# State read-outs of two batches at a time, and the last sum and stores of a fused attention and MLP kernel, on one core

## The chip, the core and the metric

The kernel runs on one core of a Trainium2 chip. The core has five engines that run side by side, each with its own queue of instructions: TensorE (PE; its weight loads are shown apart as PEld), VectorE (DVE), ScalarE (ACT), GpSimd (POOL) and SyncE (SP), which here only issues DMAs. The metric is the device time of one execution in microseconds (us). Three runs of the kernel before took 205.12, 204.68 and 204.35 us, median 204.68.

## What is computed

```python
# x: (8, 8, 512, 64) = (B, H, S, D); state: (8, 8, 32, 64) = (B, H, Ns, D)
a     = softmax(scale * x @ state.T)        # per token over the 32 states
xread = a @ state                           # (B, H, 512, 64)
a2    = softmax(scale * state @ x.T)        # per state over the 512 tokens
sread = a2 @ x                              # (B, H, 32, 64)
rows  = concat([xread, sread], axis=2)      # (B, H, 544, 64), heads then side by side: 4352 x 512
out   = gelu(rows @ w_in) @ w_out           # w_in 512 x 2048, w_out 2048 x 512
```

So there are per batch 512 token rows and 32 state rows. In the text, "state read-out" is sread: for each state a sum over the tokens of its batch, weighted with the exponentials.

## The kernel before, in words

The eight batches pass one after the other through a software pipeline that is written out by hand: instructions run on each engine in the order in which the program lists them, and the pools only add waits for buffers. For batch b the loop at line 1140 has eight slots p of two hidden tiles each; "slot 2" and the like in the diff's summary means the turn of the outer loop with b = 2, and its read-out stands at p = 5.

- **Tokens.** `scores` (L333, exponentials L340 into e), `norm` (L353 to L356, three DVE steps, the last one a product that writes a) and a DMA transpose (`atr_dma`) make the attention weights of batch b + 1 while batch b's MLP runs. `p_mm` (L441) multiplies state and w_in beforehand into P, so that gelu's argument is a product of a and P (`mm1`, L506, gelu at L513).
- **Second MLP product.** Per batch it is done by Strassen's scheme: seven products named "1" to "7" (`X`, matmuls at L623) in four PSUM banks, with sums of gelu outputs as weights (`g_sum`, L613, tile gsum, from a pool of three buffers) and sums of w_out as the other side. The results are put together by DVE adds (L642) into the halves oh, and stored by SP (`x_out`, L637). "7" is followed by the adds `c22` and `c21`, "3" by an add of its own.
- **State read-out.** At p = 5, behind X(b - 1, "3"), `p_all` runs `reads_mm` for the listed batches: 32 small matmuls per batch (L887) of e with xo, a copy of x with columns of ones for the denominators. ScalarE copies the result (sraw, L895). Then come the 32 matmuls of P for the next batch (L441), ScalarE and DVE copy the pieces of P (L925), and DVE normalises the read-out (`reads_norm`, L903 and L904, into srm). At p = 7 `srts` transposes srm on TensorE (L424) and a DVE copy puts it into XSR (L429). Batches 0 and 1 are read out before the loop; in the loop one batch is read out in each of the turns b = 2 to 5, and two, 6 and 7, in b = 6.
- **GpSimd.** It loads x (`load_x`, tile xb), makes a rearranged copy x4 for the transposes (`rearr`, L225) and the copy xo (`rearr_ones`, L235), two instructions each. xo and x4 have two buffers each, for odd and even batches. A `hold_for` is a copy of one column of a gelu output, which keeps what follows on GpSimd back until that output is there.
- **The state rows.** When all of XSR is there (b = 7), their MLP is done by the same scheme in `SR` and `R`, threaded through the last turns; R ends with adds into osb (L642) and two stores (`r_out`, L838). For SR, the weight sums of "1" and "6" are put in the two x4 buffers.
- **The end.** For batch 7 the products "5" and "3" come last, each in three pieces in PSUM banks of their own (`L5`, `L3`, matmuls at L701): tokens j = 0 whole, j = 1 in two halves. Each piece is copied or added and stored (`rows_out`, L687). The list ahead of them is:

```python
    g_sum(b, "7")
    R("7")
    X(b, "6")
    g_sum(b, "3")
    R("3")
    X(b, "7")
    c21(b)
    x_out(b, 1, left)
    L5()
    L3()
```

Of the kernel before, what the change touches and what calls it, by code (L numbers as in the profile page):

```python
# [10 lines left out]
BF16 = mybir.dt.bfloat16  # L11
# [6 lines left out]
def kernel(  # L18
# [8 lines left out]
    nc = tc.nc  # L27

    B, H, S, D = x.shape
# [15 lines left out]
    apool = ctx.enter_context(tc.tile_pool(name="apool", bufs=3))  # L45
# [36 lines left out]
    x4s = [persist.tile([128, SJ, HC, 128], BF16, name=f"x4_{i}") for i in range(2)]  # L82
# [32 lines left out]
    def load_x(b):  # L115
        xb = xin.tile([128, H, SJ * D], BF16, name="xb", tag="xb")
        nc.gpsimd.dma_start(out=xb, in_=xr[b])
        xbs[b] = xb
# [111 lines left out]
    def rearr_ones(b):  # L230
        A = atts[b]
        eng = nc.vector if b < 2 else nc.gpsimd
        src = xbs[b].rearrange("p (t c) (j d) -> p t c j d", t=2, d=D)
        for t in range(2):
            eng.tensor_copy(  # L235
                out=A.xo[:, :, :, 2 + 64 * t:66 + 64 * t].rearrange("p j c d -> p c j d"),
                in_=src[:, t],
            )
# [182 lines left out]
    def srts(bs):  # L421
        ps = ps_f.tile([128, len(bs), HC, NS], BF16, name="srT", tag="f")
        for i, b in enumerate(bs):
            nc.tensor.transpose(  # L424
                ps[:, i].rearrange("p c n -> p (c n)"),
                atts[b].srm.rearrange("q t d -> q (t d)"),
                ident,
            )
        nc.vector.tensor_copy(  # L429
            out=XSR[:, :, :, bs[0]:bs[-1] + 1], in_=ps.rearrange("p b c n -> p c n b")  # L430
        )
# [125 lines left out]
    MH = MC // 2  # L557
    NH = d_model // 2
# [23 lines left out]
    left, right = slice(0, NH), slice(NH, d_model)  # L582
# [8 lines left out]
    def g_q(b, h, k):  # L591
        return gs[b][:, MH * k:MH * k + MH, 256 * h:256 * h + 256]
# [12 lines left out]

    g_lhs = {}

    def g_sum(b, names):
        got = g_lhs.setdefault(b, {})
        for name in names:  # L610
            x, y, op = chain(name, lambda h, k: g_q(b, h, k), got)
            got[name] = apool.tile([128, MH, 256], BF16, name="gsum", tag="gsum")
            nc.vector.tensor_tensor(out=got[name], in0=x, in1=y, op=op)  # L613

    def x_lhs(b, name):
# [68 lines left out]
    def rows_out(h, js, ns, eng):  # L684
        b = B - 1
        rows = out[b * SB:b * SB + S, :].rearrange("(p j) n -> p j n", j=SJ)
        eng.dma_start(  # L687
            out=rows[:, 2 * h + js.start:2 * h + js.stop, ns], in_=xs[b, "o", h][:, js, ns]
        )
# [21 lines left out]
    def L5():  # L711
        b = B - 1
        xs[b, "s5"] = c_tile("s5")
        for ps, j, n0, n1 in l_mm("5", True):
            nc.scalar.copy(out=xs[b, "s5"][:, j, n0:n1], in_=ps)
            if n1 == NH:
                c22(b, slice(j, j + 1))
                rows_out(1, slice(j, j + 1), right, nc.sync)

    def L3():  # L720
        b = B - 1
        for ps, j, n0, n1 in l_mm("3", False):
            add(xs[b, "o", 0][:, j, NH + n0:NH + n1], ps, xs[b, "u"][:, j, n0:n1])
            rows_out(
                0, slice(j, j + 1), slice(NH + n0, NH + n1), nc.scalar if n0 else nc.sync
            )

    sr = {}
# [151 lines left out]
    def reads_mm(bs):  # L880
        sr = ftile([128, len(bs), 2, 65], "sr")
        for i, b in enumerate(bs):
            A = atts[b]
            for t in range(2):
                for j in range(SJ):
                    for c in range(HC):
                        nc.tensor.matmul(  # L887
                            sr[32 * c:32 * c + 32, i, t, :],
                            lhsT=A.e[:, 2 * j + t, 32 * c:32 * c + 32],
                            rhs=A.xo[:, j, c, 1 + 65 * t:66 + 65 * t],  # L890
                            start=(j == 0),
                            stop=(j == SJ - 1),
                        )
        raw = cpool.tile([128, len(bs), 130], FP32, name="sraw", tag="sraw")
        nc.scalar.copy(out=raw, in_=sr.rearrange("q i t d -> q i (t d)"))  # L895
        return raw

    def reads_norm(bs, raw):
        for i, b in enumerate(bs):
            A = atts[b]  # L900
            A.srm = att.tile([128, 2, D], BF16, name="srm", tag="srm")
            inv = att.tile([128, 2], FP32, name="inv", tag="inv")
            nc.vector.reciprocal(out=inv, in_=raw[:, i, 0:130:129])  # L903
            nc.vector.tensor_tensor(  # L904
                out=A.srm,
                in0=raw[:, i, 1:129].rearrange("q (t d) -> q t d", t=2),
                in1=inv[:, :].to_broadcast((128, 2, D)),
                op=ALU.mult,
            )

    def p_all(nb, bs):
        raw = reads_mm(bs)
        done = []
        for f, at in enumerate(((0, None), (None, None), (1, 3), (2, None))):
            it = iter(at)

            def tiles(shape, name):
                i = next(it)
                return ftile(shape, name) if i is None else otile(shape, name, i)

            done.append((nb, f, p_mm(nb, f, tiles)))
        for b, f, ps in done:
            for t in range(2):
                copy = nc.scalar.copy if t == 0 or f == 0 else nc.vector.tensor_copy
                copy(out=Ps[b][:, t, f * 512:(f + 1) * 512], in_=ps[t])  # L925
        reads_norm(bs, raw)

    def p_copy_s(b, f, ps):
        for t in range(2):
# [6 lines left out]
    def hold_for(b, m):  # L936
        nc.gpsimd.tensor_copy(out=hold, in_=gs[b][:, m, 0:1])
# [202 lines left out]
    for b in range(2, B):  # L1140
        nb = b + 1
        for p in range(8):
            k = 16 * b + 2 * p
            if p == 1 and nb < B:
                scores(nb, 0)
                scores(nb, 1)
            if p in (2, 3) and nb < B and (b > 2 or p == 2):
                norm(nb, p - 2)
            if p == 3 and nb + 1 < B:
                xtr_dma(nb + 1)  # L1150
            if p == 5 and nb < B:
                atr_dma(nb)
            if nb == B and p < 5:
                read_out_slot(p)
                if p == 4:
                    r_homes()
                    r_sum("56")
                continue
            if b != 2 or p != 3:
                M(k, k + 1)  # L1160
            if b == 2 and p == 2:
                M(k + 2, k + 3)
            if b == 2 and p == 1:
                w_diff("7")
            if p < 5 and nb < B:
                if p == 0:
                    g_sum(b - 1, "56")
                if p == 2:
                    g_sum(b - 1, "7")
                if p == 3:  # L1170
                    g_sum(b - 1, "3")
                if p < 4:
                    X(b - 1, "1657"[p])
                if b == 2 and p == 2:
                    norm(3, 1)
                    for x in [(2, f, p_mm(2, f, ftile)) for f in (2, 3)]:
                        p_copy(*x)
                if p == 1 and b > 2:
                    sr_w("5216"[b - 3])
            if p == 0 and b + 3 < B:  # L1180
                hold_for(b, 0)
                load_x(4 if b == 2 else b + 3)
            if p == 6 and b == 2:
                hold_for(b, 12)
                load_x(5)
            if p == 0 and nb + 1 < B:
                begin(nb + 1)
                rearr(nb + 1)
            if nb == B:
                if p == 5:  # L1190
                    R("2")
                    r_sum("73")
                    R("4")
                if p == 6:
                    R("1")
                    X(b, "2")
                    R("6")
                    R("5")
                if p == 7:
                    X(b, "4")  # L1200
                continue
            if p == 5:
                X(b - 1, "3")
                reads = (b, nb) if nb == B - 1 else (b,)
                p_all(nb, reads)
                if b == 2:
                    rearr_ones(3)
                    rearr_ones(4)
                elif nb + 1 < B:
                    rearr_ones(nb + 1)  # L1210
                X(b, "2")
            if p == 7:
                srts(reads)
                X(b, "4")
    b = B - 1
    g_sum(b, "56")
# [1 line left out]
    g_sum(b, "7")  # L1218
    R("7")
    X(b, "6")  # L1220
    g_sum(b, "3")
    R("3")
    X(b, "7")
    c21(b)
# [33 lines left out]
```

## Time and profile before

| | |
|---|---|
| median of three runs | 204.68 us |
| the profiled execution: its own time | 204.74 us |
| its span in the trace | 202.8 us |
| granted clock of TensorE, mean | 0.998 |
| PE busy | 194.0 us (96%) |
| ACT busy | 142.8 us (70%) |
| DVE busy | 140.4 us (69%) |
| POOL busy | 49.9 us (25%) |
| stores in the span | 8.91 MB written |

The page's part 4 follows the work that ended last back to the start; its shares tell which engine and which line set the time. The chain in order of time gives start, length and line of each piece of it. A timeline lists the instructions of a window: start, length, engine, line, operation, output and input, count, and in brackets how long the engine sat idle before it and what released it. "SPq" and "ACTq" rows are DMA issues; a DMA's landing is counted from its issue. Merged rows that hold several instructions run from the first one's start to the last one's end.

### The profile page before, as it was taken

What the parts mean: (1) busy time and instruction counts of PE and PEld (TensorE: products, weight loads), DVE (VectorE), ACT (ScalarE), POOL (GpSimd) and SP (SyncE); (2) the same over time, 40 slices, a digit from 0 to 9 for tenths busy, and PEclk for the clock granted to TensorE, in tenths of its full rate; (3) what the DMA queues carried; (4) which work ended last, traced back from release to release, by engine and by line L of the source; (5) the groups of instructions that cost most, each with busy time, mean ns of one, the idle gap of its engine ahead of it and who ended that gap; (6) DMA issues with size and microseconds to landing.
All of it is one profiled execution on the core that took longest, in us unless ns stands there. A gap on an engine that the chain in (4) does not pass through costs nothing.

```text
span 202.8 us, 4863 instructions
## 1 busy us (share of the span) xinstructions
PE 194.0 (96%) x2030; PEld 134.0 (66%) x2035; DVE 140.4 (69%) x235; ACT 142.8 (70%) x260; POOL 49.9 (25%) x63
## 2 busy tenths in 40 slices
PE   7799999999999999999999999999999999999990
PEld 2434544465767677767767677768767888788890
DVE  2953874889987579656996687567846787862760
ACT  3785578698994989678966896779758588555110
POOL 8963503324318434032306100400000000000000
PEclk9999999999999999999999999999999999999999
DMA  6999999987486999460997051701092010210125
GB/s 191 200 169 203 206 199 192 177 161 137 62 144 126 187 110 182 125 160 0 118 143 210 2 121 38 207 3 53 0 132 81 0 52 3 103 55 0 52 74 190
DMA packets 40582, 23.16 MB, mean 114 GB/s; under 512 B 21872, under 2 KB 39152, under 8 KB 40560
## 3 DMA queue, kind: packets, MB, share of 16 engines
q0 software_dynamic: 13984, 8.10, 29.6%
q1 hardware_dynamic: 25888, 14.36, 29.4%
q10 hardware_dynamic: 688, 0.39, 0.6%
q8 instruction: 16, 0.26, 0.5%
q14 instruction: 6, 0.05, 0.1%
HBM read 17.30 MB, written 8.91 MB: 129 GB/s over the span
## 4 chain that ended last, share of the span: by engine, by line
PE 87%; DMA 4%; POOL 4%; ACT 2%; issue 1%; DVE 0%; ACTq 0%; POOLq 0%
PE xp L623 41%; PE hp L506 27%; DMA w_in_bf<-in_moe_w_in_dram 4%; PE op L548 4%; PE sp L791 3%; PE rp L857 3%; PE op L532 2%; PE xp L701 2%; PE p_ps L441 2%; PE pt L333 2%; POOL w_in_bf L105 2%; ACT P L925 1%; PE sr L887 1%; POOL sbd L95 1%; POOL w_out_bf L113 1%
## 5 line engine op out<-in xcount | busy, mean ns | idle before, releaser
L513 ACT ACTIVATE g<-hp 128x512 bf16<-128x512 f32 x124 | 65.8, 608 | 13.7 <-PE hp L506 13.5
L506 PE MATMUL hp<-AT,P 128*128 128x512 bf16 x248 | 61.0, 379 | 0.0
L623 PEld LDWEIGHTS <-gsum 128*128 128x128 bf16 x416 | 40.5, 98 | 9.4 <-issue 0.4
L623 PE MATMUL xp<-ws,gsum 128*128 128x256 bf16 x320 | 38.2, 273 | 0.0
L506 PEld LDWEIGHTS <-P 128*128 128x128 bf16 x248 | 23.4, 98 | 20.8 <-issue 0.6
L623 PEld LDWEIGHTS <-g 128*128 128x128 bf16 x336 | 32.5, 98 | 7.1 <-issue 1.6
L623 PE MATMUL xp<-w_out_bf,g 128*128 128x256 bf16 x224 | 26.7, 272 | 0.3
L235 POOL COPY xo<-xb 128x1024 bf16<-128x1024 bf16 x12 | 13.2, 1127 | 36.3 <-PE sr L887 36.3
L613 DVE TENSOR_TENSOR gsum<-g 128x2048 bf16<-128x2048 bf16 x14 | 17.1, 1220 | 5.1 <-ACT g L513 4.5
L225 POOL COPY x<-xb 128x1024 bf16<-128x1024 bf16 x12 | 12.4, 1066 | 18.5 <-DMA xb<-in_x_dram 18.5
L646 ACT COPY c<-xp 128x512 f32<-128x512 f32 x14 | 8.3, 593 | 8.9 <-ACT g L513 3.9
L623 PE MATMUL xp<-ws,g 128*128 128x256 bf16 x112 | 13.4, 273 | 0.0
L642 DVE TENSOR_TENSOR oh<-xp,c 128x512 f32<-128x512 f32 x14 | 9.6, 685 | 5.4 <-PE xp L623 5.4
L925 ACT CAST P<-p_ps 128x512 bf16<-128x512 f32 x25 | 12.7, 606 | 0.1
L642 DVE TENSOR_TENSOR oh<-xp,u 128x512 f32<-128x512 f32 (+2 forms) x9 | 5.1, 572 | 10.6 <-PE xp L623 10.4
L548 PE MATMUL op<-w_out_bf,g 128*128 128x512 bf16 x44 | 11.1, 380 | 0.5 <-issue 0.3
L623 PE MATMUL xp<-w_out_bf,gsum 128*128 128x256 bf16 x96 | 11.5, 273 | 0.0
L613 DVE TENSOR_TENSOR gsum<-g,gsum 128x2048 bf16<-128x2048 bf16 x7 | 9.1, 1298 | 2.8 <-PE xp L623 2.8
L356 DVE TENSOR_TENSOR a<-e,ics 128x512 bf16<-128x512 bf16 x14 | 10.5, 750 | 0.5
L925 DVE CAST P<-p_ps 128x512 bf16<-128x512 f32 x15 | 9.4, 684 | 1.7 <-PE p_ps L441 1.7
L353 DVE TENSOR_REDUCE cs<-e 128x16 f32<-128x512 bf16 x14 | 9.5, 678 | 0.7 <-ACT e L340 0.7
L441 PE MATMUL p_ps<-w_in_bf,sbd 64*32 64x512 bf16 x248 | 9.2, 380 | 0.2 <-DMA w_in_bf<-in_moe_w_in_dram 0.2
(136 smaller groups left out, 248.6 us busy)
## 6 DMA issues: line engine op xcount, KB each, us to landing
xb<-in_x_dram POOLq DMA_DIRECT2D x7, 512.0 KB, 7.0
out_dram<-oh SPq DMA_DIRECT2D x14, 256.0 KB, 2.7
out_dram<-oh SPq DMA_DIRECT2D x6, 512.0 KB, 2.9
w_in_bf<-in_moe_w_in_dram POOLq DMA_DIRECT2D x6, 256.0 KB, 12.3
out_dram<-osb SPq DMA_DIRECT2D x5, 256.0 KB, 3.0
w_out_bf<-in_moe_w_out_dram POOLq DMA_DIRECT2D x4, 256.0 KB, 9.0
w_out_bf<-in_moe_w_out_dram POOLq DMA_DIRECT2D x2, 512.0 KB, 12.7
x0f<-in_x_dram SPq DMA_DIRECT2D x3, 256.0 KB, 3.8
```

The lines of the kernel that those rows point to most:

```text
L225: nc.gpsimd.tensor_copy(out=A.x4[:, :, :, 64 * t:64 * t + 64].rearrange("p j c d -> p c j d"), in_=src[:, t],)
L235: eng.tensor_copy(out=A.xo[:, :, :, 2 + 64 * t:66 + 64 * t].rearrange("p j c d -> p c j d"), in_=src[:, t],)
L353: nc.vector.reduce_sum(out=cs, in_=e4, axis=AX.X)
L356: nc.vector.tensor_tensor(out=A.a[:, :, hs].rearrange("p g (c n) -> p g c n", n=NS), in0=e4, in1=ics[:, :, :].to_broadcast((128, G, 2, NS) ...
L441: nc.tensor.matmul(ps[t][32 * c:32 * c + 32, :], lhsT=sbd[64 * t:64 * t + 64, b, c, 32 * t:32 * t + 32], rhs=w_in_bf[64 * t:64 * t + 64, c ...
L506: nc.tensor.matmul(hp, lhsT=Ps[b][:, t, m * 128:(m + 1) * 128], rhs=atts[b].AT[:, :, t, :], start=(t == 0), stop=(t == 1),)
L513: nc.scalar.activation(out=gs[b][:, m, :], in_=hp, func=AF.Gelu)
L548: nc.tensor.matmul(ops[b, j], lhsT=gs[b][:, m, j * 128:(j + 1) * 128], rhs=w_out_bf[:, m, :], start=(m == 0), stop=(m == MC - 1),)
L613: nc.vector.tensor_tensor(out=got[name], in0=x, in1=y, op=op)
L623: nc.tensor.matmul(ps[:, j - js[0], :], lhsT=lhs[:, m, 128 * j:128 * j + 128], rhs=rhs[:, m, :], start=(first and j == js[0] and m == 0), ...
L642: nc.vector.tensor_tensor(out=out, in0=x, in1=y, op=ALU.add)
L925: copy(out=Ps[b][:, t, f * 512:(f + 1) * 512], in_=ps[t])
```

## The change

- The read-outs in the loop are done for two batches at a time: (2, 3) in b = 2, (4, 5) in b = 4, (6, 7) in b = 6. In b = 3 and b = 5 there is none, and no transposes at p = 7.
- Batch 3's copy xo is now listed at p = 1 of b = 2, behind a hold on batch 2's gelu tile 2, instead of behind `p_all`. On GpSimd it still comes directly behind the x4 copies of batch 4, with the hold between.
- In the end, the sum for product "3" of batch 7 is written into x4's buffer 0 instead of a gsum buffer.
- The store of the right half behind `L5` is one of two tokens (256 KB) on SP instead of two of one token. Of the three stores of `L3`, the first and the last go out on ScalarE's queue and the second on SP; before, the first two went out on SP and the last on ScalarE's queue.

```diff
-    def g_sum(b, names):
+    def g_sum(b, names, home=None):
...
-            got[name] = apool.tile([128, MH, 256], BF16, name="gsum", tag="gsum")
+            if home is None:
+                got[name] = apool.tile([128, MH, 256], BF16, name="gsum", tag="gsum")
+            else:
+                got[name] = home
             nc.vector.tensor_tensor(out=got[name], in0=x, in1=y, op=op)
...
             if n1 == NH:
                 c22(b, slice(j, j + 1))
-                rows_out(1, slice(j, j + 1), right, nc.sync)
+        rows_out(1, slice(0, 2), right, nc.sync)
...
             rows_out(
-                0, slice(j, j + 1), slice(NH + n0, NH + n1), nc.scalar if n0 else nc.sync
+                0,
+                slice(j, j + 1),
+                slice(NH + n0, NH + n1),
+                nc.sync if j == 1 and n0 == 0 else nc.scalar,
             )
...
     def p_all(nb, bs):
-        raw = reads_mm(bs)
+        raw = reads_mm(bs) if bs else None
...
-        reads_norm(bs, raw)
+        if bs:
+            reads_norm(bs, raw)
...
+            if p == 1 and b == 2:
+                hold_for(b, 2)
+                rearr_ones(3)
...
-                reads = (b, nb) if nb == B - 1 else (b,)
+                reads = (b, nb) if b % 2 == 0 else ()
                 p_all(nb, reads)
                 if b == 2:
-                    rearr_ones(3)
                     rearr_ones(4)
...
             if p == 7:
-                srts(reads)
+                if reads:
+                    srts(reads)
                 X(b, "4")
...
-    g_sum(b, "3")
+    g_sum(b, "3", x4s[0].rearrange("p j (u c) n -> p (j u) (c n)", u=2))
```

## The prediction, made before the changed kernel ran

> **What bounds it now.** I read the page's parts 1 and 4 first, then the chain in order of time over one state read-out of one batch (slot 3) and over one of two batches (slot 6), then the timeline of the last 9 us, and last the timeline of POOL beside DVE.
>
> ```profile
> PE 87%; DMA 4%; POOL 4%; ACT 2%; issue 1%; DVE 0%; ACTq 0%; POOLq 0%
> ```
>
> TensorE is 87% of the chain that ends last. So an edit counts only where it lengthens or shortens TensorE's row of matmuls, or the end, where TensorE has stopped (197.99 us) and the span still runs to 202.8. The chain leaves TensorE inside the slots at one place, the read-out:
>
> ```profile
> 86.84 0.43 PE sr L887 x29
> ...
> 87.35 0.27 ACT sraw L895
> 87.62 0.58 ACT P L925
> 88.19 0.04 issue
> 88.23 1.91 PE xp L623 x16
> ```
> ```profile
> 150.48 0.67 PE sr L887 x57
> ...
> 151.23 0.38 ACT sraw L895
> 151.60 0.50 ACT P L925
> ...
> 152.14 1.91 PE xp L623 x16
> ```
>
> TensorE's next product (X "2") waits until ScalarE has copied the read-out (sraw) and then the first piece of P. From the first sr to X "2" it is 1.39 us for one batch, 1.66 for two. In slot 2 (65.57 to 67.02) it is 1.45, and there the chain goes through p_ps: 0.41 for its first 8 matmuls, 0.04, 0.59 of ACT P, 0.04 = 1.09 without any sr or sraw in it. That 1.09 is my row for a slot with no read-out. The end of the kernel:
>
> ```profile
> 194.48 1.23 DVE L613 TENSOR_TENSOR gsum<-g,gsum 128x2048 bf16<-128x2048 bf16 x1 [2.82 <-PE xp L623]
> ...
> 195.62 0.42 DVE L642 TENSOR_TENSOR osb<-rp,r_u 128x256 f32<-128x256 f32 x1
> 195.96 0.68 DVE L642 TENSOR_TENSOR oh<-xp,c 128x512 f32<-128x512 f32 x1
> ...
> 196.07 0.55 SPq L838 DMA_DIRECT2D out_dram<-osb  x1
> ...
> 197.12 0.39 SPq L637 DMA_DIRECT2D out_dram<-oh  x1
> ```
> ```profile
> 197.62 1.92 SPq L687 DMA_DIRECT2D out_dram<-oh  x4
> 198.01 0.29 DVE L642 TENSOR_TENSOR oh<-xp,u 128x128 f32<-128x128 f32 x1 [0.15 <-PE xp L701]
> 198.34 0.37 ACTq L687 DMA_DIRECT2D out_dram<-oh  x1
> ```
>
> The sum for product "3" waits 2.82 us for X "7", whose buffer it reuses. Two adds and two 256 KB stores queue behind it, so SP, at about 0.5 us per issue, sends its last piece (64 KB) at 199.1, although its add was done at 197.86. It lands 2.4 later, at 201.5. From 198.0 to 200.6 the DMA engines are full (share 1.01, 346 GB/s).
>
> **The tail.** In a buffer of its own the sum needs only gsum "6", so DVE runs it behind the two osb adds that end at 191.66: 191.66 to 192.89. R3 has finished by 192.70, so the osb add ends at 193.3 and its store leaves there, not at 196.07. c21 then waits only for X "7" (194.44): 194.48 to 195.17, and its store leaves at 195.2, not 197.12. The two c22 adds stay where they are, since they wait for ScalarE's copies (the last ends at 196.52): 196.98. Their stores are now one of 256 KB on SP at 197.0. The first add of product "3" ends at 197.63 and goes out on ACT's queue, the second at 197.86 on SP, the third at 198.30 (it waits for TensorE's end) on ACT at 198.34. So the last issue moves from 199.1 to 198.34, worth 0.8. L3's matmuls gain nothing, as TensorE runs L5 and L3 without a gap already.
>
> Landing. The 256 KB store issued alone at 189.89 shows data from 190.7 to 191.55 and lands 2.1 after issue, so about 0.9 before and 0.45 behind the data. After the change 0.52 MB are issued from 197.0 on; at 346 GB/s that is 1.5 us from 198.0, and the last 64 KB cannot start before 199.3 and needs 0.2. So the data end at 199.6 and land between 200.0 and 200.2. The same 64 KB on ACT's queue landed 2.5 after issue under full engines: 200.84. I take 200.2, since the row without a backlog resembles the new tail: 1.3 earlier (0.65 to 1.5).
>
> Closing waits. After 201.5 SP runs eight semaphore instructions, 0.06 apart, to 202.0. In the trace's records the first of them waits for the last store's semaphore, the lowest numbered of eight, and the others fall through. In the changed program the last store uses the highest numbered. If the list goes by number again, seven of them pass ahead of the landing: 0.4 (0 to 0.43). Tail: -1.7 (-0.65 to -1.95).
>
> On the second queue the Trainium skill (DMA: Bandwidth & Descriptors, Issuing engines are not separate DMA queues) says that all queues feed the same 16 engines, so issuing from another saves the issue time alone. By that rule the queue itself is worth little: with SP alone the last of four issues from 197.0 would leave at about 198.6. The rest of the gain is in the earlier issues, so the rule lowers what I credit to the queue, not the sum.
>
> **The read-out.** Slot 2 goes from 1.45 to 1.66 (+0.21), slot 4 from 1.40 to 1.66 (+0.26), slot 6 stays. Slots 3 and 5 go from 1.39 and 1.40 to 1.09 (-0.3 each); the fourth piece of P there needs the PSUM bank that the add of X "3" frees at 87.56, about when TensorE reaches it, so I take 1.10. Transposes: 0.11 where there are two, 0.06 where one, so nothing in sum. On ScalarE four sraw copies of 0.27 become two of 0.38, on DVE four XSR copies of 0.73 become two of 0.42 and the norms keep their number: less work, and beside TensorE's in any case. Sum -0.15 (-0.25 to 0).
>
> **What moves on POOL.** The copies xo for batch 3 keep their place behind those of batch 4 (which end at 62.03) and get one hold ahead of them. A hold is 0.19 alone, 1.20 when a DVE sum was running.
>
> ```profile
> 61.33 1.78 DVE L613 TENSOR_TENSOR gsum<-g,gsum 128x2048 bf16<-128x2048 bf16 x1
> ...
> 61.97 3.03 POOL L235 COPY xo<-xb 128x1024 bf16<-128x1024 bf16 x2
> ```
>
> Here the sum (1.22 elsewhere) waits for POOL's copy, and then POOL's next copy (1.04 elsewhere, 2.04 here) waits for the sum. The hold would wait in that copy's place, so the copies end at 65.2 to 65.4, not 65.0. Batch 3's matmuls need the first about 65.9, the second about 66.1: hidden (0 to +0.3).
>
> The xo copies of batches 5 and 7 no longer wait for the read-out in slots 3 and 5 (before: 87.16 and 129.59). They now run directly behind the x4 copies of the same batch, at 78.9 and 112.4, among DVE sums that TensorE needs:
>
> ```profile
> 77.85 1.03 POOL L225 COPY x<-xb 128x1024 bf16<-128x1024 bf16 x1
> 77.91 1.51 DVE L356 TENSOR_TENSOR a<-e,ics 128x512 bf16<-128x512 bf16 x1
> ```
>
> The softmax product (0.69 alone) waits for POOL until 78.8. Next comes gsum "7", 79.35 to 80.56, and TensorE loads it at 81.24. If a POOL copy takes its turn between the two, the sum ends at about 81.6: 0.35 of stall. If POOL's copies win both turns, it is 1.0 to 1.5, as at 96.92, where a DVE sum took 2.0 for 0.68 while two POOL copies passed. In slot 4 the second srm product stands against the batch 7 copies: the transposes need it 2.3 us behind the P copies, and one lost turn costs 0 to 0.95. Batch 7's other sums have over 1 us of slack. I take 0.35 and 0.1, by the row at 61.33, in which the turns alternate: +0.45 (0 to 2.4).
>
> The Trainium skill (SBUF — State Buffer, SBUF: two separate sides) calls the port that these two engines share an exclusive lock for a whole instruction, which goes to whoever starts first. The rows at 61.33 and 77.91 agree; at 96.92 a DVE sum that already waited was passed by a second POOL copy. Where both wait the rule would give turns in order, so 0.35 in slot 3; by the row at 96.92 it would be 1.0 or more.
>
> **Sum.** -1.7 - 0.15 + 0.45 = -1.4 against the profiled execution's 204.74 (span 202.8), which is within 0.1 of the runs' median of 204.68: **203.3**. A measurement of this kernel tells about 0.5%, 1.0 us, from no change.
>
> **Rivals.**
> - A: as worked out, 203.3. Chance 0.55.
> - B: the read-outs move without port conflicts: 204.74 - 1.85 = 202.9. For it: DVE won its turn at 61.9. Chance 0.17.
> - C: the early issues don't end the kernel earlier by more than the shorter issue row: the landing keeps its 2.5 and the closing waits stay. -0.65 - 0.15 + 0.45: 204.4, no change. For it: the fixed part of a landing was never under 2.1. Against it: the full engines at 198.0 to 200.6 are gone. Chance 0.22.
> - D: POOL's freed xo copies win every turn in slots 3 and 4, and TensorE waits 1.5 + 0.95 for gsum "7" and srm. With C's tail: 204.74 - 0.8 + 2.45 = 206.4; with A's 205.3. It decides the sign once the two waits together exceed 1.85. For it: 96.92. Against: 61.33 and 77.91, where DVE got its turn. Chance 0.06.
>
> The likeliest is A. The range takes in B and C: 202.5 to 204.8. Faster by over 0.5% (under 203.7) is B and most of A, 0.68; within it C, the rest of A and a third of D, 0.28; slower is the rest of D, 0.04.
>
> **What would show it.** The gsum "3" directly behind the osb adds near 191.7; the last issue at 198.3 on ACT's queue less all earlier shifts; a landing under 2.0 after it; fewer than three of SP's closing semaphores after that. In slots 3 and 5, 1.1 from the end of X "3" to X "2"; in slots 2 and 4, 1.66. A gap in front of X "7" in slot 3 with DVE's gsum over 1.3 would be the port. I'm wrong if the last store still lands 2.4 or later after issue, or if TensorE waits for xo in slot 2.

## The result and the profile after

The changed kernel takes **203.00 us** (median of six runs, 202.90 to 203.89); the kernel before, run beside it, takes 204.58 (six runs, 204.35 to 205.12). The ratio is 0.9927, with a 95% interval of 0.9906 to 0.9948, so it is 0.5 to 0.9% faster. The forecast was 203.3. The profiled execution took 203.18, with a span of 201.4.

Part 4 of the page, the shares of the chain by engine, now reads:

```profile
PE 91%; DVE 3%; DMA 3%; ACT 1%; SPq 0%; issue 0%
```

GpSimd has gone from the chain, but its 4% lay in the first 8.3 us before, where the work is the same in both kernels. VectorE, at 0% before, now holds 3%, and most of that lies in the loop: TensorE has got a new place where it waits, although the kernel is faster. To see what came from where, I cut each profiled execution at three points: the first matmul of the read-out in slot 2, the end of TensorE's last matmul, and the landing of the last store. All times in us.

| | start to slot 2's read-out | from there to TensorE's end | TensorE's end to the last landing | landing to the span's end | span |
|---|---|---|---|---|---|
| before | 65.50 | 132.48 | 3.52 | 1.34 | 202.84 |
| after | 65.34 | 133.06 | 2.11 | 0.90 | 201.41 |
| difference | -0.16 | +0.58 | -1.41 | -0.44 | -1.43 |

The second column is the loop, the third and fourth are the tail. The first column scatters between 65.15 and 65.94 among kernels with the same work there (two late executions, named below, left out), so its -0.16 is not an effect that these profiles can tell. The second is far steadier: seven kernels below whose loop is nearly or wholly the one before show 132.47 or 132.48. It is a much finer ruler than the whole time, and most of what follows rests on it. The tail gained 1.85, the loop lost 0.58: together 1.27, and the other 0.16 of the span is the first column's scatter.

**The tail.** The timeline of the last 10 us (start, length, engine, line, operation, output and input, count, idle time before):

```profile
192.00 1.22 DVE L616 TENSOR_TENSOR x<-g,gsum 128x2048 bf16<-128x2048 bf16 x1
...
193.15 0.42 DVE L645 TENSOR_TENSOR osb<-rp,r_u 128x256 f32<-128x256 f32 x1
...
195.68 0.39 SPq L640 DMA_DIRECT2D out_dram<-oh  x1
...
197.42 1.24 SPq L690 DMA_DIRECT2D out_dram<-oh  x2
...
198.00 1.12 ACTq L690 DMA_DIRECT2D out_dram<-oh  x2
198.43 0.29 DVE L645 TENSOR_TENSOR oh<-xp,u 128x128 f32<-128x128 f32 x1 [0.15 <-PE xp L704]
```

The sum for product "3" (the row that writes x, which is x4's buffer) runs at 192.00, not at 194.48, and no longer shows an idle time in front of it. Of the two 256 KB stores behind it, the second leaves at 195.68, where it was 197.12. TensorE ends at 198.40 and the last issue stands at 198.76 on ScalarE's queue, 0.36 behind TensorE's end; before it was 1.15 behind (199.13 against 197.98). The windows of the same trace (from:to, length, busy time of the engines, clock, DMA share, GB/s):

```profile
199.00:199.60 0.60, 0.00 (x0) 0.00 (x0) 0.00 (x0) 0.00 (x0) 0.00 (x0) 1.00 1.05 344
199.60:200.20 0.60, 0.00 (x0) 0.00 (x0) 0.00 (x0) 0.00 (x0) 0.00 (x0) 1.00 0.40 115
```

The data are through at about 199.9, and the last store lands 1.74 after its issue instead of 2.4.

**The loop.** The chain in order of time (start, length, engine, line) around the read-outs of slot 2 (two batches), slot 3 (none) and slot 4 (two):

```profile
65.41 0.78 PE sr L893 x56
...
66.21 0.31 ACT sraw L901
...
66.56 0.59 ACT P L931
...
67.19 1.91 PE xp L626 x16
...
87.19 0.77 PE p_ps L441 x24
...
87.97 0.41 PE p_ps L441 x8
88.38 1.85 PE xp L626 x16
...
109.40 1.89 DVE P L931 x3
...
111.39 1.15 DVE srm L910
...
112.66 0.95 DVE srm L910
...
113.65 0.23 PE srT L424
```

Slot 2 is 1.78 from the first sr to X "2". Slot 3 is 1.19, and all of it is TensorE's own 32 matmuls for P: there is no ScalarE row in it any more. In slot 4 the chain goes through VectorE for 4.2 us up to srT; this is most of the 3% in part 4.

Each srm product takes 0.29 alone, and 1.15 and 0.95 here, while GpSimd's copies for batch 7 run (110.37 to 114.49); srT waits for the second. A smaller wait stands in slot 3, in the timeline:

```profile
78.30 3.40 POOL L225 COPY x<-xb 128x1024 bf16<-128x1024 bf16 x2 [2.99 <-DMA xb<-in_x_dram]
...
81.65 2.48 POOL L235 COPY xo<-xb 128x1024 bf16<-128x1024 bf16 x2
...
83.15 2.05 DVE L616 TENSOR_TENSOR gsum<-g,gsum 128x2048 bf16<-128x2048 bf16 x1
...
85.26 1.64 PEld L626 LDWEIGHTS <-gsum 128*128 128x128 bf16 x16 [0.44 <-DVE gsum L616]
```

GpSimd's xo copies of batch 5 delay the sum for "3" (2.05, alone 1.22), and the loads of its weights for X "3" wait 0.44 for it; on the chain X "3" is 1.87 long there instead of 1.75 (in slot 3 before).

### The profile page after: what moved, and what is told of

Its sections match the earlier page's. It is cut to its first block, busy times and chain, and to the rows that moved or that the text cites. A ratio compares the mean times of both kernels' runs of the same rounds, so it can differ in the third digit from the quotient of the medians.

```text
span 201.4 us, 4862 instructions
## 1 busy us (share of the span) xinstructions
PE 195.8 (97%) x2035; PEld 134.1 (67%) x2035; DVE 141.6 (70%) x233; ACT 142.5 (71%) x258; POOL 51.3 (25%) x64
## 4 chain that ended last, share of the span: by engine, by line
PE 91%; DVE 3%; DMA 3%; ACT 1%; SPq 0%; issue 0%
PE xp L626 40%; PE hp L506 26%; PE op L548 5%; PE sp L797 3%; PE rp L863 3%; PE p_ps L441 3%; DMA x0f<-in_x_dram 3%; PE op L532 2%; PE xp L704 2%; PE pt L333 2%; PE sr L893 1%; DVE srm L910 1%; DVE P L931 1%; PE hp L1042 1%; PE aT_ps L374 1%; ACT P L931 1%
## 5 line engine op out<-in xcount | busy, mean ns | idle before, releaser
L616 DVE TENSOR_TENSOR gsum<-g 128x2048 bf16<-128x2048 bf16 x14 | 17.9, 1281 | 11.3 <-ACT g L513 11.3
L225 POOL COPY x<-xb 128x1024 bf16<-128x1024 bf16 x12 | 13.5, 1158 | 20.1 <-DMA xb<-in_x_dram 20.1
L548 PE MATMUL op<-w_out_bf,g 128*128 128x512 bf16 x48 | 11.8, 380 | 0.0
L944 POOL COPY hold<-g 128x1 bf16<-128x1 bf16 x6 | 3.6, 592 | 22.7 <-ACT g L513 22.7
```

Source lines behind the costliest of these rows:

```text
L225: nc.gpsimd.tensor_copy(out=A.x4[:, :, :, 64 * t:64 * t + 64].rearrange("p j c d -> p c j d"), in_=src[:, t],)
L548: nc.tensor.matmul(ops[b, j], lhsT=gs[b][:, m, j * 128:(j + 1) * 128], rhs=w_out_bf[:, m, :], start=(m == 0), stop=(m == MC - 1),)
```

## The experiments

Theory: the tail gives the whole gain, through the sum's buffer first; the paired read-outs cost, partly through port conflicts and partly by themselves. Rivals: the paired read-outs give part of the gain, or the stores' queues do. Times are medians; each ratio is to the kernel before, on the same chip, with its 95% interval. The four columns are those of the table above, from one profiled execution of each kernel.

| kernel | time | ratio | start | loop | to landing | to the end |
|---|---|---|---|---|---|---|
| e1_reads | 205.41 | 1.0031 [1.0014, 1.0047] | 65.15 | 133.04 | 3.51 | 1.32 |
| e2_tail | 203.23 | 0.9932 [0.9906, 0.9959] | 65.50 | 132.48 | 2.11 | 0.90 |
| e3_xo_late | 203.14 | 0.9919 [0.9898, 0.9940] | 65.57 | 132.60 | 2.15 | 0.89 |
| e4_rotate | 203.65 | 0.9956 [0.9941, 0.9972] | 65.31 | 133.04 | 2.09 | 1.34 |
| e5_sum | 203.31 | 0.9955 [0.9928, 0.9982] | 65.94 | 132.47 | 2.19 | 1.31 |
| e6_stores | 204.65 | 1.0003 [0.9981, 1.0024] | 65.91 | 132.47 | 3.58 | 0.96 |
| e7_one_queue | 203.03 | 0.9924 [0.9895, 0.9952] | 65.56 | 132.48 | 2.24 | 0.91 |
| e8_one_less | 204.67 | 1.0009 [0.9991, 1.0028] | 65.56 | 132.48 | 4.06 | 0.89 |
| e9_st_pool | 206.91 | 1.0110 [1.0095, 1.0125] | 66.73 | 132.48 | 4.37 | 0.90 |
| e10_no_hold | 202.65 | 0.9903 [0.9886, 0.9919] | 67.48 | 132.57 | 2.11 | 0.90 |
| e11_after_no_hold | 203.18 | 0.9927 [0.9903, 0.9951] | 65.44 | 133.05 | 2.10 | 0.89 |
| e12_tail_hold | 202.88 | 0.9905 [0.9880, 0.9930] | 67.19 | 132.48 | 2.10 | 0.91 |

The profiles of e10 and e12 are of executions that took 205.05 and 204.50, longer than all their others and late from the start; of these two, only what lies behind the first column is used.

### The two halves: e1_reads and e2_tail

e1_reads is the kernel before with the read-outs, the hold and the copies of the change, and the old tail. e2_tail is the kernel before with the tail alone:

```diff
-    g_sum(b, "3")
+    g_sum(b, "3", x4s[0].rearrange("p j (u c) n -> p (j u) (c n)", u=2))
...
-                rows_out(1, slice(j, j + 1), right, nc.sync)
+        rows_out(1, slice(0, 2), right, nc.sync)
...
-                0, slice(j, j + 1), slice(NH + n0, NH + n1), nc.scalar if n0 else nc.sync
+                0, slice(j, j + 1), slice(NH + n0, NH + n1), nc.sync if j == 1 and n0 == 0 else nc.scalar
```

> The kernel before with the read-outs in pairs and the new place of batch 3's copy, and with the old tail. Theory (the pairs lengthen TensorE's row, by the freed GpSimd copies standing in the way of DVE sums and by a pair's read-out costing more than a missing one saves): TensorE's last matmul 0.4 to 0.6 us later than before, time about 205.1 against 204.6. Rival (the pairs save 0.15 by themselves, and what the trace of the changed kernel shows beside it is an accident of when a load landed): 204.4.

> The kernel before with the new tail alone. Theory (the tail carries the whole gain and pays for the loop): 1.8 to 2.0 us under the kernel before, about 202.7, so faster than the whole change (203.0). Rival (tail and pairs each carry a part): 203.2 to 203.4, slower than the whole change.

e1_reads is slower than before, by 0.1 to 0.5%, and its loop is as long as after's: 133.04. e2_tail has the loop of before and the tail of after. So the read-outs give nothing and cost 0.56 to 0.58, and the tail gives the gain. By the whole time the change (203.00) and its better half (203.23) can't be told apart: 202.7 was expected for the tail alone, and 203.23 lies where the rival put it. It is the loop column that tells them apart.

### Taking the port conflicts out: e3_xo_late

The changed kernel, with a hold that puts the xo copies of batches 5 and 7 back to a later place on GpSimd:

```diff
                 elif nb + 1 < B:
+                    if b % 2:
+                        hold_for(b, 11)
                     rearr_ones(nb + 1)
```

> The changed kernel with the copies xo of batches 5 and 7 held back, by a hold on a late gelu tile of batches 3 and 5, to about where they stood before. Theory (the port that GpSimd and DVE share): the second srm product of slot 4 and the gsum 3 of slot 3 are no longer late, TensorE doesn't wait for them (0.40 and 0.12), 202.5. Rival (the waits come from the second norm being one more DVE step behind the copies of P, not from those copies): the wait before the transposes in slot 4 stays, 203.0.

Both waits are gone, and the loop is 132.60: 0.46 shorter than after's. In slot 4, the timeline:

```profile
111.51 1.15 DVE L910 TENSOR_TENSOR srm<-sraw,inv 128x128 bf16<-128x128 f32 x1
...
112.77 0.29 DVE L910 TENSOR_TENSOR srm<-sraw,inv 128x128 bf16<-128x128 f32 x1
...
113.37 0.28 PE L424 MATMUL srT<-ident,srm 128*128 128x128 bf16 x2
```

The first product still loses a turn to batch 7's x4 copies; the second no longer does, and nothing waits. In the whole time 203.14 against 203.00 shows no gain, where 202.5 was expected: 0.46 is less than the intervals can resolve here. What is left of the loop, 132.60 - 132.48 = 0.12, is the price of pairs without conflicts.

### What follows the last landing: e4_rotate and e8_one_less

SyncE ends the program with eight semaphore waits in a row. The prediction took it that the place of the last store's semaphore in this row sets what follows the landing. e4_rotate shifts it with one more early store in the changed kernel, e8_one_less with one fewer in the kernel before:

```diff
-            h = d_model // 2 if j == SJ - 1 else d_model
+            h = d_model // 2 if j >= SJ - 2 else d_model     # e4_rotate
+            h = d_model                                     # e8_one_less
```

> The changed kernel with one early store of batch 0 (256 KB) split into two halves on SP, so that every later DMA on the SP and ACT queues takes the next semaphore of the eight and the last store takes the lowest numbered instead of the highest. Theory (SP waits for the eight one after the other by number): from the release of the last store to the end of the span 1.3 us instead of 0.85, time 203.4. Rival (the order plays no part, or the early store is what matters): 0.85 and 203.0.

> The kernel before, whole, with two early half stores of batch 0 made one, so that every later DMA on SP's and ACT's queues takes the semaphore before; the last store, on SP, then takes the highest numbered. Theory (SP goes through the eight by number): the end 0.85 to 0.9 behind the last landing instead of 1.33, time 204.1 against 204.6, with nothing of the change in it. Rival: 1.33 and 204.6.

These are SyncE's waits behind the landing, first in the changed kernel and then in e4_rotate (line, instruction, count: durations in ns, first and last start):

```profile
L1263 SPq EVENT_SEMAPHORE  x1: 28/28/28, 200.5 to 200.5; - x1
```
```profile
L1263 SPq EVENT_SEMAPHORE  x8: 27/28/28, 200.4 to 200.9; - x8
```

One instruction is left after the landing in the one, all eight in the other. It costs 1.34 - 0.90 = 0.44 in the trace and 0.65 between the medians. In e8_one_less the same shift works the other way: 0.89, as expected. But the time did not fall, as the landing came 0.54 later behind TensorE's end (4.06 for 3.52) and took it back. That was a miss. The issue of SP's last store took 0.86 there instead of 0.40. By windows of 0.4 from TensorE's end, the share of the DMA engines falls to 0.29 from 2.4 on and rises again to 0.47 from 2.8 on; in the kernel before it is 0.60 and then 0.04.

### Which part of the tail: e5_sum, e6_stores and e7_one_queue

e5_sum is the kernel before with only the first pair of lines of e2_tail's diff (the sum's buffer); e6_stores is the kernel before with only the others (the merged store and the queues). e7_one_queue is e2_tail with all last stores on SP:

```diff
-                0, slice(j, j + 1), slice(NH + n0, NH + n1), nc.sync if j == 1 and n0 == 0 else nc.scalar
+                0, slice(j, j + 1), slice(NH + n0, NH + n1), nc.sync
```

> The kernel before with the buffer for the last sum alone; the stores stay on their queues and in their sizes, and the last store (ACT's queue) takes the lowest numbered semaphore. Theory (the sum's wait is what put the stores late; once it is gone even SP's five issues are out by 198.1): last landing about 200.1 to 200.3 as with the whole tail, end 1.3 behind it, 203.2 to 203.4. Rival (the number of issues on SP sets the end, whenever they become ready): last landing 200.9 to 201.3, 204.0 or more.

> The kernel before with the merged store and the queues alone; the sum still waits for X 7. The last issue is then at 198.34 as in the whole tail. Theory (full DMA engines, from the late stores of 0.5 MB, hold back the last landing): landing 200.7 to 201.0, 2.4 or more after its issue, end 0.85 behind it, 203.6 to 203.9. Rival (a landing is a fixed time after its issue): 200.1, 202.8 to 203.0.

> The kernel before with the new tail, but with all its stores on SP's queue. Theory (a second queue saves the issue time of one store): last issue at 198.6 instead of 198.34, last landing about 200.35, 0.25 later than with two queues, 203.1 to 203.4. Rival (two queues move data at the same time and land sooner): the landing 0.5 or more later.

The buffer alone brings the landing to 2.19 behind TensorE's end, 1.33 of the 1.41. The stores alone bring nothing in time: 204.65 (ratio 0.998 to 1.002), where 203.6 to 203.9 was expected. In the trace they gain 0.38 behind the landing (0.96 for 1.34), but the landing itself is no earlier (3.58 for 3.52). Their timeline shows why:

```profile
194.89 1.23 DVE L613 TENSOR_TENSOR gsum<-g,gsum 128x2048 bf16<-128x2048 bf16 x1 [2.82 <-PE xp L623]
...
196.47 0.55 SPq L838 DMA_DIRECT2D out_dram<-osb  x1
...
197.54 0.39 SPq L637 DMA_DIRECT2D out_dram<-oh  x1
198.03 1.04 SPq L687 DMA_DIRECT2D out_dram<-oh  x2
198.07 1.04 ACTq L687 DMA_DIRECT2D out_dram<-oh  x2
```

The last issue is at 198.75, as early behind TensorE's end (0.36) as after the change. But the sum still waits its 2.82, so the two 256 KB stores behind it leave at 196.47 and at 197.54 and meet the others. The windows of this kernel:

```profile
200.20:200.80 0.60, 0.00 (x0) 0.00 (x0) 0.00 (x0) 0.00 (x0) 0.00 (x0) 1.00 1.10 364
200.80:201.40 0.60, 0.00 (x0) 0.00 (x0) 0.00 (x0) 0.00 (x0) 0.00 (x0) 1.00 0.42 122
```

The engines are still full at 200.8, where the changed kernel is done at 199.9, and the last landing comes 3.2 after the last issue. (That store, on ScalarE's queue, takes 2.8; the other 64 KB, issued on SP at 198.58, takes 3.4 and lands last.) So here an earlier issue alone is worth nothing behind a full backlog; the earlier data are the gain. Next to the buffer, the merged store and the queues give 0.08 at the landing (2.11 for 2.19) and 0.41 through the semaphore (1.31 behind the landing in e5_sum, 0.90 in e2_tail). With a single queue the last issue is 0.56 behind TensorE's end instead of 0.36, and the landing 2.24 instead of 2.11: the second queue gives 0.13 in the trace, about half of the 0.25 expected.

The Trainium skill (DMA: Bandwidth & Descriptors, Issuing engines are not separate DMA queues) says that another issuing engine saves only the time of the issue. The 0.13 agrees with it.

### A probe of the late landing: e9_st_pool

In e8_one_less one SP store fewer came with a later landing. To see whether the number of SP's instructions does that, one early load of the kernel before goes to GpSimd's queue, which shifts the semaphores and leaves SP as it was:

```diff
-    nc.scalar.dma_start(out=st_f, in_=st_rows[:, 0, :, :])
+    nc.gpsimd.dma_start(out=st_f, in_=st_rows[:, 0, :, :])
```

> The kernel before with its very first load (the state of batch 0) issued from GpSimd's queue instead of ScalarE's. SP's list of instructions is unchanged, but every DMA on SP and ACT takes the semaphore before, and the last store the highest numbered. The start of the kernel changes with it, so the reading is the trace's end: from TensorE's last matmul to the last landing, and from there to the end of the span. Theory (closing waits by number; the late landing of the run with one store fewer came from a stall on SP whose place moves with its number of instructions): 3.5 as before and then 0.85 to 0.9 instead of 1.34. Rival (the last store lands later whenever it uses the highest semaphore): 4.0 and 0.9.

The landing is late again, 4.37, with 0.90 after it, so SP's count is not the cause. (The start is also 1.2 longer, since the moved load is early work; that is half of the 2.3 by which this kernel is slower than before.) The issue of the last store is long again. SP's issues of the last four stores in e8_one_less and in e9_st_pool (shortest/median/longest in ns; the longest is the last store's):

```profile
L687 SPq DMA_DIRECT2D out_dram<-oh x4: 353/394/865, 197.9 to 199.4; - x4
```
```profile
L687 SPq DMA_DIRECT2D out_dram<-oh x4: 353/389/1272, 199.0 to 200.5; - x4
```

Against the 0.40 of before, the issues are 0.46 and 0.87 longer, and the landings are 0.54 and 0.85 later. So the late landing goes with a long last issue; what makes that issue long is not shown. In the old tail the two kernels whose last store has the highest semaphore land late, the ones with the lowest land at 3.5. In the new tail both stand at 2.1. Why stays open.

### The hold and the late load: e10_no_hold, e11_after_no_hold and e12_tail_hold

After the change, batch 5's x load lands later: GpSimd's x4 copies start at 78.30, before at 76.65. e10_no_hold is e3_xo_late without the hold ahead of batch 3's copies, e11_after_no_hold the changed kernel without it. e12_tail_hold is e2_tail with this hold and the earlier listing:

```diff
             if p == 1 and b == 2:
-                hold_for(b, 2)
                 rearr_ones(3)
```

> The run with the xo copies of batches 5 and 7 held back, but without the hold ahead of batch 3's copies. Theory (the hold only waits for the port in the place of the first copy): the copies of batch 3 end at the same time to 0.1, slot 2 and the time as with the hold, 203.1. Rival (the hold puts the copies back and slot 2's read-out waits for them, which is why it took 1.78 and not 1.66): slot 2 0.1 shorter, 203.0.

> The changed kernel without the hold ahead of batch 3's copies, and nothing else. Theory (the hold is what makes batch 5's load of x land 1.7 us later, as all five traces with it have shown and the seven without it have not): batch 5's x4 copies start 11.2 to 11.4 us behind slot 2's first read-out matmul, not 13.0; the copies xo that follow them then stand against gsum 7 instead of gsum 3, and TensorE's wait for gsum 3 in slot 3 is gone; the wait before the transposes in slot 4 (0.40) stays. Time 202.8 to 203.0. Rival (the pairs or the place of the xo copies make the load late, and the one trace without hold was an exception): 13.0, and 203.0.

> The kernel before with the new tail and with batch 3's copies listed as in the change, behind the hold, but with the read-outs of one batch each as before. Theory (the hold makes the load late, without any pair): batch 5's x4 copies start 13.0 us behind slot 2's first read-out matmul, not 11.2. The xo copies wait there for the read-out of slot 3, so the late x4 copies alone cost TensorE nothing: 203.0 to 203.2, as with the tail alone. Rival (the pairs make it late): 11.2.

Batch 3's copies end in time with or without the hold, and slot 2's stretch, counted here from the read-out's very first matmul, is 1.84 without it (e10) and 1.87 with (e3): the hold costs nothing. Counted from slot 2's read-out, the x4 copies of batch 5 start here:

| before | e2, e5 to e9 | e12 (hold, no pairs) | after | e1 | e3 | e4 | e11 (no hold, pairs) | e10 (no hold, pairs) |
|---|---|---|---|---|---|---|---|---|
| 11.15 | 11.13 to 11.26 | 11.45 | 12.96 | 12.82 | 13.36 | 12.86 | 13.10 | 11.32 |

So the late load does not need the hold: in e11 it is late without it, at 13.10 where 11.2 to 11.4 was expected. It goes with the paired read-outs in five of the six kernels that have them; e10 is the exception. With the hold and no pairs it is early in e12, 11.45 where 13.0 was expected, but e10 and e12 are the two executions that were late from the start, so they alone settle nothing. Counted from slot 2's read-out the load is issued 0.3 later after the change, and it takes 7.3 instead of 5.8 to land. What slows it, and why e10's profiled execution escaped, stays open. By the medians e10 and e12 are the shortest of all, 202.65 and 202.88; both beat the kernel before, and neither interval lies clear of the changed kernel's.

## Why the prediction was right, point by point

The time was right within 0.3. Of the sum of -1.4, tail and loop together give -1.27 in the traces (-1.85 and +0.58, forecast -1.7 and +0.30); the span's -1.43 looks closer only by the first column's -0.16. The tail was 0.15 better than forecast, the loop 0.28 worse, and the two made up for each other in part: that is luck.

- **The sum's buffer, last issue, landing: -1.3; measured -1.41.** The mechanism was as put: sum at 192.00, c21's store at 195.68, last issue 0.36 behind TensorE's end (TensorE ends 0.42 later than before, and these times with it). e5_sum shows that the buffer alone gives 1.33. The landing was predicted 1.86 behind the issue and took 1.74.
- **The closing waits: -0.4; measured -0.44.** e4_rotate undid it: 1.34 again.
- **The read-outs: -0.15; measured +0.12.** This is the step that failed, and its sign with it. (The terms as listed add up to -0.13.) The pairs in slots 2 and 4 were priced at +0.21 and +0.26, by slot 6; without port conflicts they cost +0.34 and +0.30 (e3_xo_late, 1.79 and 1.70 against 1.45 and 1.40). The slots with none were priced at -0.3 each; they save 0.20 each up to X "2" on the chain (1.19 and 1.20 for 1.39 and 1.40), and 0.06 more in X "2" itself (1.85 for 1.91 where nothing stops TensorE ahead of it), so 0.26. That is +0.64 - 0.52 = +0.12. Most of the miss is in the pairs, 0.17; the slots with none give 0.08. The row chosen for a slot with none, 1.09, held the first 8 matmuls for P and then ScalarE; in the slot itself TensorE's own 32 matmuls take 1.18, and they are the longer way. For the pairs slot 6 fitted slot 4 within 0.04, but slot 2 only within 0.13. This is slot 2 in e3_xo_late:

```profile
65.64 0.79 PE sr L893 x63
...
66.45 0.31 ACT sraw L901
...
66.80 0.59 ACT P L931
...
67.43 1.91 PE xp L626 x16
```

From the first sr to sraw it is 0.81 and 0.78 in slots 2 and 4 (0.75 in slot 6), and from sraw to X "2" 0.98 and 0.92 (0.91). Slot 2 was 0.05 longer than slot 4 already before the change, which a price by slot 6 leaves out; the rest of its excess is not explained.
- **The port: +0.45; measured +0.46** (after against e3_xo_late). Size right, places wrong: 0.35 was put on the sum for "7" in slot 3 and 0.1 on srm in slot 4. The sum for "7" did take 2.06, but started at 78.75, as the late x load had left VectorE alone before it, and ended ahead of X "7"; the sum for "3" was hit instead, for 0.12 on the chain. srm in slot 4 lost a turn twice (1.15 and 0.95 for 0.29) and cost the rest, about 0.34, within the 0 to 0.95 given. The nearly equal total is chance.
- **The hold and batch 3's copies: hidden; right.** The hold took 1.19 and the copies ended at 65.01, as before.

Of the rivals, B's time (202.9) lies even nearer to 203.00 than the forecast, so the time alone does not rule it out. B (no conflicts) fell with e1_reads and e3_xo_late, C (the landing keeps 2.5 and the closing waits stay) with the tail of the trace after, and D with the loop column: TensorE lost 0.46 where D needed 2.45. C's late landing came true in e6_stores, though, where only the issues moved.

## What to carry to other kernels

Cut the trace at points where one stage ends and compare stages: here the whole time could not tell the change from its better half, and the loop column could: it repeated to 0.01. In a tail, bring the data of the big stores forward, and not just the last issue: here the small last stores landed 2.8 and 3.4 after their issue behind two late 256 KB stores (e6_stores), and 1.7 and 2.0 where those had left earlier (after). When work is taken away from some turns and doubled in others, price the freed turn by what remains there as the longest way (here TensorE's own matmuls), and not by a row in which another engine still stood in the chain; and price the doubled turn from its own row before the change, not from another turn's.

## What the runs showed of the hardware

- Behind the last landing SyncE runs eight semaphore waits, 0.06 apart, in fixed order. With the last landing on the first of them, 1.31 to 1.34 pass from the landing to the end (before, e1, e4, e5); with it on the last, 0.89 to 0.91; in e6_stores, where it is on the last but one, 0.96. One early DMA more or less changes it (e4, e8, e9).
- The two last 64 KB stores landed 1.7 and 2.0 after their issue on engines that were running dry (after), 2.4 and 2.5 behind a backlog (before), and 2.8 and 3.4 in e6_stores, where they were issued earlier behind the same late stores.
- A small product on VectorE (128x128 from an f32 operand, 0.29 alone) took 0.94 to 1.15 while GpSimd copied (slot 4 after the change). With GpSimd's xo copies moved away (e3_xo_late) the second one took 0.29 again.
